# Another first batch, and branch hints on TensorE in the second MoE, in a fused FFT-mixer and two-MoE kernel

## The chip, the cores and the metric

The kernel runs on one NeuronCore of a Trainium2 chip, as one program and one launch. The metric is the device time of that launch in microseconds (us); lower is better. All engines of the core work in it: TensorE (PE in the rows; its weight loads are PEld), VectorE (DVE), ScalarE (ACT), GpSimd (POOL) and the queue of SyncE (SP), which only starts DMAs. DMAs are also started from ScalarE's and GpSimd's queues.

## What is computed

The input `x` has 8 batches of 3072 tokens of width 256. Three things follow each other:

1. A mixer along the sequence: `X = rfft(x)`, then a complex matrix product with `w_r`, `w_i` (256 x 256) and a bias, a soft threshold, and `irfft`:

```
Yr = Xr @ w_r - Xi @ w_i + b_r
Yi = Xr @ w_i + Xi @ w_r + b_i
Yr = sign(Yr) * max(|Yr| - 0.01, 0)        # and Yi alike
y  = irfft(Yr + 1j * Yi)
```

2. A dense MoE layer for all 24576 tokens, with 2048 hidden units: `h = relu(y @ w_in); x = h * h @ w_out`. Its two weights come as float64 and must be turned into float32 pairs on the chip ("decoding").

3. A routed layer: a token whose product with `w_skip` is positive goes to one of 8 experts (1024 hidden units), chosen by the largest of 8 logits; `out = x + gate * (relu(x @ w1[e]) @ w2[e])`. The other tokens are passed through.

Every product that has to be exact to float32 is made of pairs: an operand is split into a high part that TensorE's float32r reads without loss and a low rest, and three matmuls (high x high, high x low, low x high) are added up in PSUM. So an operand costs a rounding copy (ScalarE) and a subtraction (VectorE or GpSimd).

## The kernel before

The transform of a batch is done in two steps of small matrices. Step one (`s1_chunk`, 16 chunks `c`) multiplies by a 96 x 96 matrix and writes the result to a DRAM buffer `scr1`. Step two works on 12 groups `k` of two 128-row blocks each; a group passes through:

- `grp_read`: a DMA of 256 KB from `scr1` into `grd`;
- `grp_a`: four matmuls with `fw` into a PSUM bank, split by ScalarE into `xth` and by `grp_a2` (VectorE) into the rest `xtl`. `grp_a2` also forms `xs`, the sum of real and imaginary part, which `grp_a3` splits in turn (ScalarE, GpSimd);
- `grp_b`: the complex product. Three real products are used in place of four: of the sum with one matrix, and of each part with another. That is 18 matmuls of 256 columns into two banks, `both` and `own`;
- `grp_b2` (VectorE): bias plus `both`, plus `own`, the threshold (`mc` is the clamped value, `md` the difference). The four subtractions of 64 rows that give `md` also move real and imaginary rows into one 128-row operand. Then `mhi` (ScalarE) and `mlo` (GpSimd);
- `grp_c`: the inverse step, two times three matmuls with `iv` (pairs), copied by ScalarE to `v` and written by a DMA to `scr2`.

`sb_read` and `sb_tile` read `scr2` back and make the last inverse step; their result feeds the MoE.

The first batch has nothing to hide behind, so it is written out by hand inside a block in which the order of the code is the order on each engine: 16 chunks, then a loop over `k` from 0 to 14 in which iteration `k` issues `grp_a(k)`, a mixed sequence of `grp_b2(k - 2)`, a step of the decoder and `grp_a2(k)`, then `grp_a3(k)`, `grp_c(k - 3)` and `grp_b(k - 1)`. `mixed` takes the pieces of its generators in turn. After the loop come `sb_read`, seven chunks of the second batch and one `sb_tile`.

The decoder (`decode_a`, `decode_b`) works through 32 pieces of 128 x 512 words, of which the groups' loop takes one per iteration. On a piece VectorE makes `deca`, `decb`, `decw`, `decp` with integer operations, `decf` is built up by ScalarE and GpSimd, or on VectorE where `own(k)` says so, VectorE zeroes tiny values with `decw`, and the result is split into two parts, the rounding copy on VectorE or ScalarE, again by `own(k)`, the rest on GpSimd.

From then on a list of steps rules the order: for each tile of 384 tokens and each of 16 pieces `m` of the hidden layer, `l1` and, two steps later, `l2`, with the transform of the next batch put into fixed slots (`fft_schedule`). The scheduler is free outside of hand-written blocks and may move what does not depend on the rest to an earlier place.

The last stage is the routed layer, again in a hand-written order. The number of tokens of an expert is known on the chip only, so the code of an expert is a chain of up to 12 nested conditions, one per tile of 256 tokens:

```
def tiles(i):
    with tc.If((fast0 if e == 0 and i == first else n) > i * T2) as cond:
        ...
        moe2(e, *place(e, i), ...)
        if i + 1 < STATIC:
            tiles(i + 1)
```

Every engine runs each condition as a compare-and-branch of its own (L1033). While an expert has tokens left, the branch falls through to the next tile; at its end the branch is taken, past the tiles that are not needed, to the code of the next expert. Three tiles of the first expert are made ahead of the chain.

## Time and profile before

| | |
|---|---|
| median of 3 runs | 3532.19 us (3532.07 to 3536.48) |
| the profiled execution: its own time | 3548.67 us |
| its span | 3546.8 us |
| PE busy | 3431.1 us, 97% of the span |
| DVE busy | 2341.6 us, 66% |
| ACT busy | 2174.0 us, 61% |
| POOL busy | 831.0 us, 23% |

The profiled execution took 16.5 us longer than the median of the runs, and its span is 1.9 us shorter than its own time. The shares are averages over stages with different limits: in the page's line of slices PE stands at 9 (90% or more) from the third slice to the end, but at 6 and 7 in the first two, where DVE stands at 7 and 9. So the first slices and the last stage are to be read apart from the rest.

### The profile page before, as it was taken

How to read it: one execution, taken by the hardware profiler on the slowest of the kernel's cores; microseconds unless marked ns; L12 is line 12 of the kernel's file. 1: busy time of each engine (PE TensorE's matmuls, PEld its weight loads, DVE VectorE, ACT ScalarE, POOL GpSimd, SP SyncE). 2: the span in 40 equal slices, each digit the busy share in tenths (PEclk: the TensorE clock that was granted, in tenths of full speed). 3: DMA queues.
4: the chain of work that ended last, by engine and by line, in shares of the span. 5: the costliest groups of instructions: out<-in, count | busy, mean ns of one | idle time of the engine just before them, and what ended most of it. 6: DMA issues, size and time to landing. Idle time of an engine off the chain costs nothing. (4 is left out here: it accounts for less than half of the span.)

```text
span 3546.8 us, 69418 instructions
## 1 busy us (share of the span) xinstructions
PE 3431.1 (97%) x24974; PEld 3360.0 (95%) x24974; DVE 2341.6 (66%) x6851; ACT 2174.0 (61%) x4669; POOL 831.0 (23%) x808
## 2 busy tenths in 40 slices
PE   6799999999999999999999999999999998999998
PEld 4599999999999999999999999999999998999998
DVE  7956777766776677767766766777765654444444
ACT  3377766766776676676676766666777743333332
POOL 5501111221122112212221222011101234333333
PEclk8799999999999999999999999999999999999999
DMA  6532222222222122222221222111111112213221
GB/s 218 155 94 75 76 64 66 65 70 63 63 71 65 54 74 63 65 60 66 68 63 59 69 67 67 44 52 53 40 47 37 41 34 81 84 46 95 71 73 39
DMA packets 190870, 244.44 MB, mean 69 GB/s; under 512 B 32807, under 2 KB 142382, under 8 KB 190466
## 3 DMA queue, kind: packets, MB, share of 16 engines
q1 hardware_dynamic: 164770, 197.63, 19.4%
q0 software_dynamic: 18800, 32.64, 3.4%
q10 hardware_dynamic: 6896, 9.11, 0.7%
q8 instruction: 214, 3.51, 0.4%
q14 instruction: 190, 1.56, 0.2%
HBM read 124.76 MB, written 115.82 MB: 68 GB/s over the span
## 5 line engine op out<-in xcount | busy, mean ns | idle before, releaser
L461 DVE TENSOR_TENSOR glo<-r,ghi 128x384 fp32r<-128x384 f32 x1024 | 622.8, 609 | 615.4 <-ACT ghi L460 608.0
L122 PE MATMUL ps_acc<-wout,ghi 128*128 128x256 f32 x6144 | 917.8, 284 | 6.2 <-ACT ghi L460 3.6
L122 PE MATMUL ps_h<-yhi,win 128*128 128x384 f32 x4096 | 889.7, 339 | 0.4 <-ACT r L456 0.4
L122 PEld LDWEIGHTS ps_acc<-wout,ghi 128*128 128x128 f32 x6144 | 850.6, 189 | 22.2 <-ACT x L475 5.6
L486 DVE SCALAR_TENSOR_TENSOR junk<-x,wg 128x256 f32<-128x256 f32 x1701 | 812.2, 477 | 86.4 <-ACT x L475 44.1
L456 ACT ACTIVATE r<-ps_h 128x384 f32<-128x384 f32 x1024 | 503.6, 492 | 591.4 <-PE ps_h L122 493.3
L122 PEld LDWEIGHTS ps_h<-yhi,win 128*128 128x128 f32 x4096 | 675.7, 189 | 3.8 <-ACT r L456 2.0
L457 ACT ACTIVATE r<-r 128x384 f32<-128x384 f32 x1024 | 538.1, 525 | 31.7
L122 PE MATMUL ps_acc<-wout,glo 128*128 128x256 f32 x3072 | 537.7, 282 | 4.8 <-DVE glo L461 3.5
L460 ACT CAST ghi<-r 128x384 fp32r<-128x384 f32 x1024 | 525.5, 513 | 22.8 <-POOL wout L105 2.6
L122 PE MATMUL ps_h<-ylo,win 128*128 128x384 f32 x2048 | 525.8, 338 | 0.0
L122 PEld LDWEIGHTS ps_acc<-wout,glo 128*128 128x128 f32 x3072 | 439.0, 188 | 10.2 <-DVE glo L461 9.5
L630 POOL DMA_INDIRECT slots<-val,idx x192 | 191.5, 997 | 806.3 <-DVE idx L628 723.6
L122 PEld LDWEIGHTS ps_h<-ylo,win 128*128 128x128 f32 x2048 | 373.2, 188 | 0.0
L883 ACT ACTIVATE h2h<-ps_h 128x256 fp32r<-128x256 f32 x271 | 104.4, 385 | 301.7 <-PE ps_h L122 207.8
L122 PE MATMUL ps_acc<-w,h2h 128*128 128x256 f32 x1600 | 263.7, 287 | 3.8 <-ACT h2h L883 3.1
L105 POOL TENSOR_TENSOR mlo<-md,mhi 128x512 fp32r<-128x512 f32 x96 | 125.1, 1303 | 560.4 <-ACT mhi L412 523.0
L884 DVE SCALAR_TENSOR_TENSOR h2l<-ps_h,h2h 128x256 fp32r<-128x256 f32 x271 | 114.6, 424 | 207.1 <-ACT h2h L883 165.4
L122 PEld LDWEIGHTS ps_acc<-w,h2h 128*128 128x128 f32 x1600 | 220.1, 191 | 4.8 <-ACT h2h L883 4.0
L105 POOL TENSOR_TENSOR xlo<-xraw,xhi 96x512 fp32r<-96x512 f32 x96 | 128.3, 1337 | 394.0 <-ACT xhi L174 349.6
L105 POOL TENSOR_TENSOR xtl<-xs,xth 128x256 fp32r<-128x256 f32 x96 | 78.9, 822 | 486.7 <-ACT xth L372 241.8
L388 PE MATMUL ps_fft<-wm,xth 128*128 128x256 f32 x1152 | 188.8, 287 | 2.4 <-ACT xth L372 2.4
(172 smaller groups left out, 4474.7 us busy)
## 6 DMA issues: line engine op xcount, KB each, us to landing
grd<-scr SPq DMA_DIRECT2D x96, 256.0 KB
d<-scr SPq DMA_DIRECT2D x64, 384.0 KB
out_dram<-x SPq DMA_DIRECT2D x192, 128.0 KB
x1s<-x SPq DMA_DIRECT2D x192, 128.0 KB
xraw<-in_x_dram SPq DMA_DIRECT2D x125, 192.0 KB
scr<-v SPq DMA_DIRECT2D x84, 256.0 KB
scr<-s1o SPq DMA_DIRECT2D x106, 192.0 KB
wraw<-in_moe_w_dram SPq DMA_DIRECT2D x32, 256.0 KB
```

Source lines behind the costliest of these rows:

```text
L105: return engine.tensor_tensor(out=out, in0=a, in1=b, op=ALU.subtract)
L122: nc.tensor.matmul(out=out, lhsT=lhs[a], rhs=rhs[b], start=first and (a, b) == (0, 0), stop=last and pairs is then)
L388: nc.tensor.matmul(out=out_, lhsT=x[i][:, c, kb, :], rhs=w[n][j][:, kb, :], start=not (kb or i or j), stop=bool(low and kb))
L456: nc.scalar.activation(out=g, in_=p, func=AF.Relu)
L457: nc.scalar.activation(out=g, in_=g, func=AF.Square)
L460: nc.scalar.copy(out=hi, in_=g)
L461: st["step"] = nc.vector.tensor_tensor(out=lo, in0=g, in1=f32(hi), op=ALU.subtract).ins
L486: nc.vector.scalar_tensor_tensor(out=junk, in0=o, scalar=1.0, in1=st["wg"][:, e, :], op0=ALU.mult, op1=ALU.mult, accum_out=st["lg", b][:, ...
L630: ins = nc.gpsimd.indirect_dma_start(out=slots[:], out_offset=bass.IndirectOffsetOnAxis(ap=idx, axis=0), in_=val, in_offset=None, bounds_c ...
L883: nc.scalar.activation(out=hi, in_=p, func=AF.Relu)
L884: nc.vector.scalar_tensor_tensor(out=lo, in0=p, scalar=0.0, in1=f32(hi), op0=ALU.max, op1=ALU.subtract)
```

## The change

In the first batch alone (`b == 0`):

- `grp_b` uses four real products again. With the weights held as (-w_i, w_r, w_i), one matmul of 512 columns makes a part's share of both outputs; there are 12 of them in a group, into one bank. `xs` and its split fall away (`grp_a3` is not called), and so does VectorE's second addition in `grp_b2`.
- `grp_b2` makes `md` with one subtraction of 128 x 512 and leaves real and imaginary rows where they are. In their place `grp_c` multiplies half-height operands (64 of the 128 rows), with matrices `iv0` that are laid out for that: 12 matmuls of 256 columns in a group in place of 6, alternating between rows 0 to 63 and 64 to 127, into two banks, and two copies to `v` in place of one.
- The weights are split in two parts: `split_first` for the first batch, and `split_mix` (sum and difference of the weights, for the three products of the later batches) among the MoE's first steps. The matrices `iv` of the later batches are loaded into the buffers of `iv0` by 8 more DMAs of 384 KB on GpSimd's queue.
- `w_r` and `w_i` are loaded after chunk 5, the biases after the first two `grp_read`; three chunks of the second batch are loaded inside the loop.

In the decoder: `decw` is made by ScalarE (a square, compared with the square of the old bound), the rounding copy is always on ScalarE, and `own(k)` holds for even `k` below 8 and above 20. Four of the first 16 chunks' copies go from ScalarE to VectorE.

In the routed layer: each tile issues, on TensorE alone, a hint for the branch of the next tile, with the outcome computed from the number of tokens, after the fifth piece of the hidden layer.

```diff
-            ins = nc.scalar.copy(out=o.rearrange("p a b -> p (a b)"), in_=p[:96, :])
+            if early and not b and c > 8 and c % 2:
+                nc.vector.tensor_copy(out=o.rearrange("p a b -> p (a b)"), in_=p[:96, :])
+            else:
+                nc.scalar.copy(out=o.rearrange("p a b -> p (a b)"), in_=p[:96, :])
...
+        def split_first(stage):
+            for n, t in zip((1, 2), stage):
+                nc.scalar.copy(out=wm[:, n, 0], in_=t)
+                sub(nc.vector, wm[:, n, 1], t, f32(wm[:, n, 0]))
+            nc.vector.tensor_scalar(out=wm[:, 0], in0=f32(wm[:, 2]), scalar1=-1.0, scalar2=None, op0=ALU.mult)
...
-            return k < 6 or k > 20
+            return k % 2 == 0 and (k < 8 or k > 20)
...
-            ve.tensor_scalar(out=w, in0=high, scalar1=0x7FFFFFFF, scalar2=None, op0=ALU.bitwise_and)
+            nc.scalar.activation(out=f32(w), in_=high.bitcast(F32), func=AF.Square)
...
-            nc.vector.scalar_tensor_tensor(out=f, in0=w, scalar=float(0x38100000), in1=f, op0=ALU.is_ge, op1=ALU.mult)
-            yield
-            if own(k):
-                nc.vector.tensor_copy(out=dst[0], in_=f)
-            else:
-                nc.scalar.copy(out=dst[0], in_=f)
+            nc.vector.scalar_tensor_tensor(out=f, in0=f32(w), scalar=(1.125 * 2.0 ** -15) ** 2, in1=f, op0=ALU.is_ge, op1=ALU.mult)
+            yield
+            nc.scalar.copy(out=dst[0], in_=f)
...
-            both = bank(b, "fft", 3)[:, :D]
+            both = bank(b, "fft", 3)[:, :D] if b else None
             own = bank(b, "fft", 3).rearrange("p (c e) -> p c e", c=2)
-            for out_, c, n in ((both, 2, 0), (own[:, 0, :], 1, 2), (own[:, 1, :], 0, 1)):
+            if b:
+                todo = ((both, 2, wm[:, 1], None), (own[:, 0, :], 1, wm[:, 0], 0), (own[:, 1, :], 0, wm[:, 2], 1))
+            else:
+                todo = ((own, (0, 1), (wm[:, 1:3], wm[:, 0:2]), None),)
+            for out_, c, w, first in todo:
+                terms = [(c, w, kb) for kb in range(2)] if b else [(c[n], w[n], kb) for n in range(2) for kb in range(2)]
...
-            nc.vector.tensor_tensor(out=t, in0=both.unsqueeze(1).broadcast_to([128, 2, D]), in1=bias, op=ALU.add)
+            whole, part = (both.unsqueeze(1).broadcast_to([128, 2, D]), both) if b else (own, own[:, 1, :])
+            nc.vector.tensor_tensor(out=t, in0=whole, in1=bias, op=ALU.add)
...
-            nc.vector.tensor_tensor(out=t, in0=own, in1=t, op=ALU.add)
-            yield
+            if b:
+                nc.vector.tensor_tensor(out=t, in0=own, in1=t, op=ALU.add)
+                yield
...
+            else:
+                sub(nc.vector, d, t, c)
...
+                p = [psum(f"acc{(2 * k + g) % 3}", [128, 512], 1)[:, :D] for g in range(2)]
+                order = [(i, a, c) for c in range(2) for i in range(2) for a in range(2 - c)]
+                for n, (i, a, c) in enumerate(order):
+                    for g in range(2):
+                        s = slice(64 * g, 64 * g + 64)
+                        nc.tensor.matmul(out=p[g], lhsT=iv[a][s, 2 * k + i, :], rhs=m[c][s, i, :], start=n == 0, stop=n == len(order) - 1)
+                for g in range(2):
+                    nc.scalar.copy(out=v[:, g, :], in_=p[g])
...
-                if k < NK:
-                    grp_a3(0, k)
...
+                if i == 2 and NB > 1:
+                    staged = load_mix(nc.sync)
+                if i in (18, 21, 24, 27) and NB > 1:
+                    load_iv((i - 18) // 3, "iv_")
+                if i == 12 and NB > 1:
+                    split_mix(staged)
...
-                with tc.If((fast0 if e == 0 and i == first else n) > i * T2) as cond:
+                more_rows = (fast0 if e == 0 and i == first else n) > i * T2
+                with tc.If(more_rows, preferred_fallthrough_block=True, label=f"tile{e}_{i}" if i > first else None) as cond:
...
+                        between[4].append(lambda: tc.mark_branch_hint_location(f"tile{e}_{i + 1}", n > (i + 1) * T2, {ET.PE}))
```

The order of the instructions, at three places. VectorE in the loop over the groups, one iteration, before:

```order
L396 TENSOR_TENSOR mt<-ps_fft,bias 128x512
L260 TENSOR_SCALAR deca<-raws 128x256
L400 TENSOR_TENSOR mt<-ps_fft,mt 128x512
L264 SCALAR_TENSOR_TENSOR decb<-raws,deca 128x256
L402 TENSOR_SCALAR mc<-mt 128x512
L266 TENSOR_SCALAR decw<-raws 128x256
L268 TENSOR_SCALAR decp<-decb 128x256
L282 SCALAR_TENSOR_TENSOR decf<-decw,decf 128x256
L105 TENSOR_TENSOR xtl<-ps_h,xth 128x4x2x64
L105 TENSOR_TENSOR md<-mt,mc 64x256 x4
L356 TENSOR_TENSOR xs<-ps_h,xs 128x256
```

and now:

```order
L421 TENSOR_TENSOR mt<-ps_fft,bias 128x512
L272 TENSOR_SCALAR deca<-raws 128x256
L428 TENSOR_SCALAR mc<-mt 128x512
L276 SCALAR_TENSOR_TENSOR decb<-raws,deca 128x256
L107 TENSOR_TENSOR md<-mt,mc 128x512
L281 TENSOR_SCALAR decp<-decb 128x256
L295 SCALAR_TENSOR_TENSOR decf<-decw,decf 128x256
L107 TENSOR_TENSOR xtl<-ps_h,xth 128x4x2x64
```

The second addition (L400), `decw` and `xs` are gone, the four pieces of `md` are one, and `md` stands ahead of `xtl`.

TensorE at the same place, from the inverse step of one group to the first matmuls of another, before:

```order
L122 MATMUL ps_acc_659<-mhi,iv_88 128x256
L122 MATMUL ps_acc_659<-mhi,iv_89 128x256
L122 MATMUL ps_acc_659<-mlo,iv_88 128x256
L388 MATMUL ps_fft<-wm,xth 128x256 x4
L388 MATMUL ps_fft<-wm,xtl 128x256 x2
L340 MATMUL ps_h<-fw,grd 128x128 x4
```

(the first three lines stand twice in a group, the next two three times) and now, from the middle of the inverse step:

```order
L461 MATMUL ps_acc_676<-mhi,iv_89 128x256
L461 MATMUL ps_acc_677<-mhi,iv_89 128x256
L461 MATMUL ps_acc_676<-mlo,iv_88 128x256
L461 MATMUL ps_acc_677<-mlo,iv_88 128x256
L409 MATMUL ps_fft<-wm,xth 128x512 x8
L409 MATMUL ps_fft<-wm,xtl 128x512 x4
L350 MATMUL ps_h<-fw,grd 128x128 x4
```

The inverse step alternates between two banks, and the complex product has fewer and wider matmuls.

TensorE in a tile of the routed layer, between two pieces of the hidden layer, now:

```order
L124 MATMUL ps_h<-xt2h,w_00_34827 128x256
L124 MATMUL ps_h<-xt2h,w_01_34828 128x256
L124 MATMUL ps_h<-xt2l,w_00_34827 128x256 x2
L1097 REGISTER_ALU
L1136 BRANCH_PREFETCH_HINT
L124 MATMUL ps_acc_38329<-w_00_34829,h2h 128x256
```

The two rows without a matmul are new; before, the matmuls follow one another there.

## Rows read from the trace of the kernel before

**Rows 1.** Busy time by stretch: stretch, length, engines busy (instructions), PEclk, DMA share, GB/s

```profile
0.00:39.50 39.50, 19.24 (x32) 5.85 (x32) 24.99 (x59) 13.12 (x22) 15.82 (x25) 0.87 0.89 287
53.50:120.40 66.90, 47.76 (x287) 42.74 (x286) 66.25 (x128) 26.64 (x63) 42.88 (x50) 0.86 0.40 126
120.40:134.90 14.50, 8.50 (x42) 7.39 (x41) 13.98 (x26) 3.57 (x8) 8.15 (x9) 0.74 0.40 127
134.90:169.20 34.30, 24.98 (x62) 13.41 (x62) 28.34 (x69) 10.40 (x21) 16.75 (x21) 0.65 0.70 211
2934.70:3537.80 603.10, 574.48 (x4728) 571.97 (x4728) 272.86 (x625) 202.94 (x486) 215.16 (x210) 0.97 0.24 68
```

**Rows 2.** Timeline of DVE, one group: start, us, engine, line, operation, shapes

```profile
83.39 0.68 DVE L105 TENSOR_TENSOR xtl<-ps_h,xth 128x512 fp32r<-128x512 f32 x1
83.99 2.14 DVE L105 TENSOR_TENSOR md<-mt,mc 64x256 f32<-64x256 f32 x4
86.16 0.42 DVE L356 TENSOR_TENSOR xs<-ps_h,xs 128x256 f32<-128x256 f32 x1
86.50 0.68 DVE L396 TENSOR_TENSOR mt<-ps_fft,bias 128x512 f32<-128x512 f32 x1
87.10 1.18 DVE L260 TENSOR_SCALAR deca<-raws 128x256 uint32<-128x256 uint32 x1
88.20 0.68 DVE L400 TENSOR_TENSOR mt<-ps_fft,mt 128x512 f32<-128x512 f32 x1
...
89.14 0.95 DVE L402 TENSOR_SCALAR mc<-mt 128x512 f32<-128x512 f32 x1
90.01 0.41 DVE L266 TENSOR_SCALAR decw<-raws 128x256 uint32<-128x256 uint32 x1
```

**Rows 3.** Timeline of POOL, in that group

```profile
86.86 1.27 POOL L105 TENSOR_TENSOR mlo<-md,mhi 128x512 fp32r<-128x512 f32 x1 [1.88 <-ACT mhi L412]
```

**Rows 4.** Timeline of PE: a forward step, and a step of the first MoE

```profile
54.29 1.05 PE L340 MATMUL ps_h<-fw,grd 128*128 128x128 f32 x8
...
179.32 0.87 PE L122 MATMUL ps_h<-yhi,win 128*128 128x384 f32 x4
...
180.38 0.88 PE L122 MATMUL ps_acc<-wout,ghi 128*128 128x256 f32 x6
...
181.45 0.86 PE L122 MATMUL ps_h<-yhi,win 128*128 128x384 f32 x4
```

**Rows 5.** Timeline from the last group to the first MoE's steps

```profile
134.91 0.62 ACT L412 CAST mhi<-md 128x512 fp32r<-128x512 f32 x1 [3.04 <-DVE md L105]
...
147.93 3.70 PE L438 MATMUL ps_fft<-sb,d 96*128 96x96 f32 x16 [4.25 <-DMA sb<-in_sb_dram]
...
169.22 1.13 DVE L461 TENSOR_TENSOR glo<-r,ghi 128x384 fp32r<-128x384 f32 x1
```

**Rows 6.** Timeline of PE: the first matmuls of two tiles that follow one another

```profile
3242.83 0.64 PE L122 MATMUL ps_h<-xt2h,w 128*128 128x256 f32 x4
...
3254.68 0.63 PE L122 MATMUL ps_h<-xt2h,w 128*128 128x256 f32 x4
```

**Rows 7.** Waits of PE from 3000 to 3530: total us, times, longest

```profile
PE ps_h L122 <- issue: 10.0, 2, 7.0
PE ps_fft L122 <- PEq L1033: 6.9, 2, 3.8
PE ps_h L122 <- PEq L1033: 6.3, 2, 3.2
PE ps_h L122 <- DVEq L1033: 3.5, 1, 3.5
```

**Rows 8.** The branch's line from 3255 to 3275: duration ns min/median/max, first and last start

```profile
L1033 PEldq COMPARE_BRANCH  x3: 65/197/3563, 3265.4 to 3269.5; - x3
```

**Rows 9.** Busy time in the 10 us after a wait (first and last of seven)

```profile
3014.16:3024.16 10.00, 10.00 (x64) 10.00 (x65) 4.63 (x9) 4.33 (x10) 2.73 (x3) 0.73 0.56 173
...
3524.22:3534.22 10.00, 10.00 (x72) 10.00 (x73) 2.55 (x6) 2.69 (x7) 2.89 (x3) 0.83 0.19 40
```

More of the change, by code (lines that the diff above doesn't have):

```diff
@@ L79, in _constants @@
     s1 = s1.reshape(96, 96)
+    iv0 = iv.reshape(NG // 2, 2, 2, 64, 128).transpose(1, 3, 0, 2, 4).reshape(128, NG, 128)
     iv = iv.reshape(NG, 128, 128).transpose(1, 0, 2)
@@ L82, in _constants @@
     out = {}
-    for name, m in (("s1", s1), ("iv", iv)):
+    for name, m in (("s1", s1), ("iv", iv), ("iv0", iv0)):
         hi = _round12(m)
@@ L204, in split_mix @@
             sub(nc.vector, diff, i, r)
-            for n, t in enumerate((r, diff, total)):
+            for n, t in ((0, total), (2, diff)):
                 nc.scalar.copy(out=wm[:, n, 0], in_=t)
@@ L211, in load_fw, with load_iv @@
             queue.dma_start(out=fw[:, 6 * q:6 * q + 6], in_=A["fw"][:, 6 * q:6 * q + 6])
-        def load_iv(q):
+        def load_iv(q, name="iv0_"):
             for i, k in enumerate(("hi", "lo")):
-                nc.gpsimd.dma_start(out=iv[i][:, 6 * q:6 * q + 6], in_=A["iv_" + k][:, 6 * q:6 * q + 6])
+                nc.gpsimd.dma_start(out=iv[i][:, 6 * q:6 * q + 6], in_=A[name + k][:, 6 * q:6 * q + 6])
         win = [const.tile([128, 2, DFF], F32R, name=f"win{i}", tag=f"big{4 + i}") for i in range(2)]
@@ L346, in grp_a @@
             xv = [t[:, :2].rearrange("p c k (g j) -> p (k g) c j", g=2) for t in x]
-            xs = sbuf("xs", [128, 4, 64], F32)
             nc.scalar.copy(out=xv[0], in_=pv)
-            nc.scalar.copy(out=xs, in_=pv[:, :, 0, :])
+            xs = None
+            if b:
+                xs = sbuf("xs", [128, 4, 64], F32)
+                nc.scalar.copy(out=xs, in_=pv[:, :, 0, :])
             st["xt", b, k] = x, xv, xs, pv
@@ L355, in grp_a2 @@
             yield
-            nc.vector.tensor_tensor(out=xs, in0=pv[:, :, 1, :], in1=xs, op=ALU.add)
+            if b:
+                nc.vector.tensor_tensor(out=xs, in0=pv[:, :, 1, :], in1=xs, op=ALU.add)
             real = None
@@ L364, in grp_a2 @@
                     nc.vector.tensor_scalar(out=first, in0=f32(first), scalar1=0.0, scalar2=None, op0=ALU.mult)
-                first = xs.rearrange("p (k g) j -> p k g j", g=2)[:, :, 0, 0:1]
-                nc.vector.tensor_scalar(out=first, in0=first, scalar1=0.0, scalar2=None, op0=ALU.mult)
-            st["xt", b, k] = x, xs, real
+                if b:
+                    first = xs.rearrange("p (k g) j -> p k g j", g=2)[:, :, 0, 0:1]
+                    nc.vector.tensor_scalar(out=first, in0=first, scalar1=0.0, scalar2=None, op0=ALU.mult)
+            st["xt", b, k] = (x, xs, real) if b else (x, real)
         def grp_a3(b, k):
@@ L374, in grp_a3, with first_bins @@
             st["xt", b, k] = x, real
+        def first_bins(out_, real, c):
+            for h in range(2):
+                mm3(nc, out_[0:1], [real[:, i, c, h:h + 1] for i in range(2)], [wm[:, 1, i, h, :] for i in range(2)], False, False)
         def grp_b(b, k):
             x, real = st.pop(("xt", b, k))
-            w = [[wm[:, n, i] for i in range(2)] for n in range(3)]
-            both = bank(b, "fft", 3)[:, :D]
+            both = bank(b, "fft", 3)[:, :D] if b else None
             own = bank(b, "fft", 3).rearrange("p (c e) -> p c e", c=2)
-            for out_, c, n in ((both, 2, 0), (own[:, 0, :], 1, 2), (own[:, 1, :], 0, 1)):
+            if b:
+                todo = ((both, 2, wm[:, 1], None), (own[:, 0, :], 1, wm[:, 0], 0), (own[:, 1, :], 0, wm[:, 2], 1))
[3 more added lines that the diff above has]
+                terms = [(c, w, kb) for kb in range(2)] if b else [(c[n], w[n], kb) for n in range(2) for kb in range(2)]
                 for low, pairs in enumerate((((0, 0), (0, 1)), ((1, 0),))):
-                    for kb in range(2):
-                        if low and kb and real is not None and n:
-                            for h in range(2):
-                                mm3(nc, out_[0:1], [real[:, i, 1 - c, h:h + 1] for i in range(2)], [t[:, h, :] for t in w[0]], False, False)
+                    for n, (c_, w_, kb) in enumerate(terms):
                         for i, j in pairs:
-                            nc.tensor.matmul(out=out_, lhsT=x[i][:, c, kb, :], rhs=w[n][j][:, kb, :],
-                                             start=not (kb or i or j), stop=bool(low and kb))
+                            rhs = w_[:, j, kb, :] if b else w_[:, :, j, kb, :]
+                            nc.tensor.matmul(out=out_, lhsT=x[i][:, c_, kb, :], rhs=rhs, start=not (n or i or j),
+                                             stop=bool(low and n == len(terms) - 1))
+                        if low and n == 0 and real is not None:
+                            for r in range(2) if not b else () if first is None else (first,):
+                                first_bins(out_ if b else own[:, r, :], real, r)
             st["p", b, k] = both, own
@@ L730, in fft_mixer_moe_kernel @@
                     grp_b(0, k - 1)
-                if NB > 1 and NK - 1 <= k < NK + 3:
-                    ld(1, k - NK + 1)
+                if NB > 1 and k in (4, 6, 8):
+                    ld(1, k // 2 - 2)
+            if NB > 1:
+                ld(1, 3)
             sb_read(0, 0)
```

37 lines of the change are left out of this document (22 added, 15 removed).

## The prediction

> **What bounds the kernel now.** I read the busy time by stretch first, since the page's averages hide the stages [rows 1]. From 53.5 to 120.4 us, where nine groups of the first batch pass, VectorE is busy 66.25 of 66.90 us and TensorE 47.76: the loop is VectorE's, 66.90 / 9 = 7.43 us a group. In the last stage, from 2934.7 to 3537.8, TensorE is busy 574 of 603 us at a granted clock of 0.97: that stage is TensorE's, with holes. Between the two, some 2700 us of dense MoE are TensorE's without holes, and the change leaves them alone. So two stages decide, each by its own limit.
>
> The timeline of VectorE shows where a group's 7.4 us go [rows 2]; start to start is what an instruction costs there, since VectorE never idles. `md` takes 83.99 to 86.16 = 2.17 us, `xs` 0.34, the second addition (L400) 0.61, `decw` some 0.3 of its 0.41. `deca` takes 1.10 from its start at 87.10 to the next start, and ends at 88.28: just after GpSimd's `mlo`, which ran from 86.86 to 88.13 [rows 3]. So part of VectorE's time is waiting for GpSimd inside an instruction.
>
> In the routed layer one tile costs TensorE 3254.68 - 3242.83 = 11.85 us when nothing is in the way [rows 6]. The stage has 4728 matmuls [rows 1], a tile 100 (48 per layer and 4 transposes), so 47 tiles, which would take 557 us. It took 603: 46 us are lost. The waits of TensorE name where [rows 7]: 10.0 + 6.9 + 6.3 + 3.5 = 26.7 us in seven waits, one at the end of each expert but the last. The rows name L1033, the branch, and the branch itself shows it [rows 8]: it takes 65 ns when it falls through, and 3563 ns once, where it is taken. So a taken branch stops TensorE's sequencer for 3.6 us, of which some 3.3 are seen as a wait (the sequencer runs a little ahead). After each such wait the engine is slow as well: in the 10 us behind it the granted clock is 0.73 in the first of seven cases and 0.83 in the last [rows 9], where 1.00 is 2.4 GHz and 0.50 is 1.2 GHz; that is 10 x 0.27 = 2.7 and 1.7 us lost, 2.2 on the mean. Seven times 2.2 and 26.7 make 42 of the 46 us.
>
> **The loop over the groups.** VectorE loses `xs` 0.34, L400 0.61, `decw` 0.33, and `md` shrinks from 2.17 to one 128 x 512 operation, priced like `xtl`, 0.60 (83.39 to 83.99) [rows 2]. Left: 7.43 - 1.28 - 1.57 = 4.6 us for the group shown, if the waits for GpSimd stay as long as they are.
>
> TensorE gets more work. From the first MoE's steps: 9 matmuls of 256 columns in 181.45 - 180.38 = 1.07, so 0.119 each, 6 of 384 in 1.06, so 0.177 [rows 4]; on that line 512 columns cost 0.235 (an estimate; no row has that width in float32r). The complex product goes from 18 x 0.119 = 2.1 to 12 x 0.235 = 2.8. The forward step stays at about 0.9 [rows 4]. The inverse step goes from 6 to 12 matmuls: no row has half-height ones, so they lie between 6 x 0.119 = 0.7, as if two halves ran at once, and 12 x 0.119 = 1.4. I take 1.4, the nearest row being a whole matmul of that width. Sum: 0.9 + 2.8 + 1.4 = 5.1 at full clock. TensorE therefore becomes the limit of the loop, not VectorE. The clock was 0.86 there [rows 1], with TensorE idle a third of the time; with hardly any idle time I take 0.95: 5.4 us a group. The Trainium skill (TensorEngine Tiling (Array Packing), Key Properties) says that tiles of different rows run matmuls in parallel, and that a change of the tiling mode drains the engine. By it the inverse step would cost 0.7 and two drains, the loop would be VectorE's again at 4.6 to 4.8 us, and the sum 6 us better; no row here can show it.
>
> ScalarE had 26.6 of 66.9 us in the loop [rows 1]: it loses `xs` and its split and gets a square and a second copy, about the same. GpSimd had 42.9, 4.8 a group; it loses the rest of `xs` and gets 8 DMA starts in all, so it stays under 5.4. Two of these DMAs wait for TensorE's inverse step in front of `mlo`; the step is due earlier anyway, so I cost them nothing, and if they block, GpSimd is the next limit.
>
> Nine groups gain 9 x (7.43 - 5.4) = 18. The first two groups gain little (1). The end, 14.5 us [rows 1], shrinks to two complex products, one inverse step and VectorE's last chain, 2.8 + 1.4 + 2.8 + 0.6 + 0.4 + 0.6 = 8.7, a gain of 6. Together 25.
>
> **Ahead of the loop.** Three raw pieces of 256 KB no longer stand ahead of the first group's read: 0.8 MB at 287 GB/s [rows 1], 2.7 us. Against it, squares in ScalarE's queue wait for raw pieces and hold chunk copies behind them, though VectorE takes four of those. I take 1.5 gained, between 3 lost and 3 gained.
>
> **Behind the loop.** From the last group to the first `glo` are 34.3 us [rows 1, 5], in which the eleven last pieces are decoded on VectorE. Now a piece costs it `deca` 1.10, `decb` 0.33, `decp` 0.2 and the zeroing 0.34, about 2.1 with half an `own` operation: 23, and 2.4 for four operations of the new `split_mix`, which the scheduler pulls forward to here. So 26 in place of 34. ScalarE comes close to that now with its squares, copies and rounding, so I take a gain of 6, not 8. The chain of data cannot gain more than this: from `mhi` at 134.91 to the last inverse step at 147.93, 13 us [rows 5], a DMA to DRAM and back, stays. The dense MoE is costed at nothing.
>
> **The routed layer.** If the hint makes the target ready in time, the branch costs what one that falls through does. The hint stands behind the fifth of eight pieces, about half a tile or 6 us ahead of the branch, longer than the 3.6 us. Its two instructions cost about what a branch does, 65 ns, 47 times, hidden as long as the sequencer is ahead. I keep 9.5 of the 42 us: one of the seven waits was 7.0 long [rows 7], two blocks in a row, of which the hint covers one (3.7 and 2.2 for the slow clock), and one was ended by VectorE's own branch (3.5), which gets no hint. Gain 32.
>
> **The sum.** 25 + 1.5 + 6 + 32 = 64.5 us. Against the profiled execution's 3548.7 that gives 3484; the runs' median is 16.5 lower, and I carry the difference over: 3532.2 - 64.5 = **3468 us**.
>
> **Rivals.**
> *The hints do nothing.* For it: no hint ran in the kernel before, so nothing shows that one shortens a branch; against it: a hint knows the target 6 us ahead. The loop's 32.5 us stay: 3500. The Trainium skill (Runtime: NRT & Kernel Launch, Instruction fetch mechanics) says that instructions are prefetched in sequence only and that a taken branch out of the present blocks stalls for a fetch; the 3563 ns agree with the second half, and by the first this rival would be right. Chance 0.17.
> *The pairs run at once*, 4.7 us a group: 9 x 0.7 = 6 better, 3462. Chance 0.15.
> *The loop is held* by a clock that stays low, by GpSimd's queue or by the 3 MB that the 8 extra loads add to it: 6.6 us a group, 11 us lost, and 2 more ahead or behind: 3481. For it: 0.86 and 0.40 of DMA share [rows 1] while less was asked. Chance 0.12.
> *Slower.* The block that a hint fetches takes the place of the one that TensorE runs into next. Then tiles that fall through stall as the taken ones did, 3.3 us and 2.2 of slow clock, up to 40 times: 40 x 5.5 = 220, less 32.5 of the first batch: 3720. It decides against the change from six such stalls on (32.5 / 5.5). Against it: the hint is computed from the count, and says "not taken" on these 40. Chance 0.03.
>
> **How the numbers follow.** My forecast, 3450 to 3486 on its own, has 0.50; with the two cases inside that stretch, 0.77. The range reaches up to the first rival and a little over it, and down to the pairs with all seven waits gone: 3446 to 3506. A measurement of this kernel tells 0.2%, about 7 us, from no change. Faster 0.95, the same 0.02, slower 0.03.
>
> **What would show it.** In the loop: starts of `xtl` 5.4 us apart, TensorE without idle time, VectorE with some. 12 matmuls of the inverse step in 1.4 us, or in 0.7. `glo` for the first time near 136 in place of 169. In the last stage: taken branches on TensorE well under 1 us, waits behind L1033 nearly gone, the clock at 1.00. I am wrong if the taken branch still takes 3.5 us, if a branch that falls through takes more than 65 ns, or if `xtl` stays at 7 us.

## The result: 0.85% faster, under half of what was forecast

| | before | changed |
|---|---|---|
| median | 3533.4 us (4 runs) | 3503.6 us (4 runs: 3501.6 to 3507.5) |
| ratio | 1 | 0.9916, 95% interval 0.99 to 0.9932 |
| profiled execution, span | 3546.8 us | 3505.7 us |

The gain is 30 us where 64.5 were forecast, and 3504 lies in the upper end of the range. The stages of the changed kernel first, with the same columns as [rows 1]: the prologue, nine groups of the loop, the end of the loop, the stretch from the last `mhi` to the first `glo`, the routed layer.

```profile
0.00:38.70 38.70, 21.80 (x32) 6.38 (x32) 16.29 (x40) 13.68 (x29) 12.77 (x22) 0.81 0.84 263
56.10:105.00 48.90, 46.50 (x296) 38.12 (x295) 42.12 (x74) 25.16 (x63) 37.27 (x45) 0.97 0.71 217
105.00:113.60 8.60, 6.11 (x39) 4.12 (x37) 8.46 (x13) 3.59 (x11) 6.61 (x8) 0.97 0.70 193
113.60:152.50 38.90, 26.20 (x68) 14.48 (x69) 26.36 (x56) 17.88 (x44) 21.91 (x30) 0.63 0.78 227
2914.50:3496.00 581.50, 565.16 (x4724) 563.72 (x4725) 274.08 (x624) 204.13 (x486) 217.18 (x211) 0.99 0.24 71
```

Nine groups take 48.90 us, 5.43 each (before 7.43), and TensorE is busy 46.50 of them. The end of the loop takes 8.6 in place of 14.5. But the stretch behind the loop has grown from 34.3 to 38.9 us, and its DMA share stands at 0.78. The timeline of TensorE in a group, and its first complex product:

```profile
46.03 3.75 PE L409 MATMUL ps_fft<-wm,xth 128*128 128x512 f32 x8 [3.52 <-DVE real L376]
...
67.42 1.05 PE L350 MATMUL ps_h<-fw,grd 128*128 128x128 f32 x8
68.40 0.74 PE L461 MATMUL ps_acc<-mhi,iv 64*128 64x256 f32 x8
68.97 0.40 PE L461 MATMUL ps_acc<-mlo,iv 64*128 64x256 f32 x4
69.30 2.14 PE L409 MATMUL ps_fft<-wm,xth 128*128 128x512 f32 x8
71.28 1.10 PE L409 MATMUL ps_fft<-wm,xtl 128*128 128x512 f32 x4
```

Twelve half-height matmuls take 0.90 us (68.40 to 69.30). The first part of the first complex product takes 3.75 us where the same eight matmuls later take 2.14; the granted clock was 0.50 (1.2 GHz) there, behind a wait of 3.52 us. The stretch behind the loop, from the timeline of all engines:

```profile
113.60 0.38 SPq L197 DMA_DIRECT2D stage<-in_w_r_dram  x1
113.61 0.62 ACT L442 CAST mhi<-md 128x512 fp32r<-128x512 f32 x1 [1.63 <-DVE md L107]
117.50 0.54 POOL L227 DMA_DIRECT2D iv<-in_iv_hi_dram  x1 [0.67 <-PE ps_acc L461]
122.95 0.33 SPq L469 DMA_DIRECT2D d<-scr  x1
128.31 3.70 PE L479 MATMUL ps_fft<-sb,d 96*128 96x96 f32 x16 [4.47 <-DMA sb<-in_sb_dram]
141.12 0.18 DVE L627 TENSOR_SCALAR val<-tokid 128x24 uint32<-128x24 f32 x1 [5.96 <-DMA tokid<-in_tokid_dram]
152.49 1.09 DVE L502 TENSOR_TENSOR glo<-r,ghi 128x384 fp32r<-128x384 f32 x1
```

The chain of data starts 21.3 us earlier than before (113.61 against 134.91 [rows 5]), but the first `glo` only 16.7 earlier (152.49 against 169.22; the prediction looked for it near 136). From the eighth `glo` to the 512th the lead is a steady 14.5 to 15.0 us.

In the routed layer, the waits of TensorE and its branches at two ends of an expert (the waits' columns are us in all, times, longest; the branch's row has the smallest, median and largest duration in ns; PEq and DVEq are the sequencers of TensorE and VectorE, and "issue" is time in which the engine waited for nothing that the profile shows):

```profile
PE ps_h L124 <- DVEq L1084: 9.2, 4, 3.6
PE ps_fft L124 <- PEq L1084: 3.2, 1, 3.2
PE ps_h L124 <- issue: 2.6, 1, 2.6
PE ps_fft L124 <- DVEq L1084: 1.1, 1, 1.1
```

```profile
L1084 PEldq COMPARE_BRANCH  x3: 65/192/380, 3161.0 to 3162.6; - x3
L1084 PEldq COMPARE_BRANCH  x3: 73/186/3761, 3407.4 to 3411.7; - x3
```

The taken branch, 3563 ns in [rows 8], takes 380 ns. That holds for seven of nine; a second branch in a row takes 2065, and the seventh, near 3407, still 3761. The seven waits are 16.1 us in place of the 26.7 of [rows 7], and five of them now name VectorE's sequencer (DVEq).

### The profile page after: what moved, and what is told of

Its sections match the earlier page's. It is cut to its first block, busy times and chain, and to the rows that moved or that the text cites. A ratio compares the mean times of both kernels' runs of the same rounds, so it can differ in the third digit from the quotient of the medians.

```text
span 3505.7 us, 69465 instructions
## 1 busy us (share of the span) xinstructions
PE 3421.7 (98%) x24974; PEld 3344.7 (95%) x24974; DVE 2302.6 (66%) x6739; ACT 2184.7 (62%) x4711; POOL 829.1 (24%) x812
## 5 line engine op out<-in xcount | busy, mean ns | idle before, releaser
L124 PEld LDWEIGHTS ps_acc<-wout,glo 128*128 128x128 f32 x3072 | 439.6, 189 | 11.2 <-DVE glo L502 10.5
L409 PE MATMUL ps_fft<-wm,xth 128*128 128x256 f32 (+1 forms) x1104 | 187.6, 294 | 3.5 <-DVE real L376 3.5
L107 POOL TENSOR_TENSOR xtl<-xs,xth 128x256 fp32r<-128x256 f32 x84 | 67.8, 807 | 485.0 <-ACT xth L386 229.9
```

Of the source, the lines that this page charges most:

```text
L107: return engine.tensor_tensor(out=out, in0=a, in1=b, op=ALU.subtract)
L124: nc.tensor.matmul(out=out, lhsT=lhs[a], rhs=rhs[b], start=first and (a, b) == (0, 0), stop=last and pairs is then)
L409: nc.tensor.matmul(out=out_, lhsT=x[i][:, c_, kb, :], rhs=rhs, start=not (n or i or j), stop=bool(low and n == len(terms) - 1))
```

## Experiments

Each ratio is to the kernel before on the same chip, with its 95% interval. "First glo" (its start) and "routed" (from the start of the last `glo` to the end) are from the run's profile, in us.

| run | median | before there | ratio | first glo | routed |
|---|---|---|---|---|---|
| changed kernel | 3503.6 | 3533.4 | 0.9916 (0.99 to 0.9932) | 152.5 | 637.9 |
| h_only | 3517.4 | 3536.4 | 0.995 (0.9936 to 0.9963) | 170.9 | 635.9 |
| no_hints | 3533.4 | 3536.4 | 0.9994 (0.9985 to 1.0003) | 153.2 | 662.4 |
| hints3 | 3505.7 | 3536.4 | 0.9917 (0.9903 to 0.9931) | 150.7 | 638.8 |
| hold_val | 3505.7 | 3536.4 | 0.9922 (0.9908 to 0.9935) | 150.1 | 636.6 |
| before_again | 3535.5 | 3538.0 | one run | 169.4 | 654.7 |
| hold_iv | 3501.7 | 3538.0 | 0.9896 (0.9879 to 0.9912) | 145.3 | 637.7 |
| hold_mix | 3504.2 | 3538.0 | 0.9904 (0.9888 to 0.9921) | 153.0 | 636.3 |
| no_pairs | 3505.1 | 3538.0 | 0.9904 (0.9888 to 0.9921) | 152.5 | 637.3 |
| read_q | 3508.2 | 3539.1 | 0.9916 (0.9902 to 0.9929) | 153.4 | 637.8 |
| late_hint | 3522.3 | 3539.1 | 0.996 (0.9947 to 0.9973) | 151.4 | 654.2 |
| best | 3505.9 | 3539.1 | 0.9904 (0.9889 to 0.9919) | 147.6 | 638.3 |
| before12 | 3557.5 | 3548.7 | 1.0029 (1.0019 to 1.0039) | 170.0 | 672.0 |
| h_only12 | 3539.7 | 3548.7 | 0.9977 (0.9967 to 0.9986) | 171.1 | 655.2 |
| after_same | 3508.6 | 3539.2 | 0.9916 (0.9902 to 0.9929) | 154.7 | 638.7 |
| hold_iv2 | 3501.8 | 3539.2 | 0.9895 (0.988 to 0.991) | 148.4 | 635.9 |

### The two halves of the change

h_only is the kernel before with the hints:

```diff
-                with tc.If((fast0 if e == 0 and i == first else n) > i * T2) as cond:
+                more_rows = (fast0 if e == 0 and i == first else n) > i * T2
+                with tc.If(more_rows, preferred_fallthrough_block=True, label=f"tile{e}_{i}" if i > first else None) as cond:
...
+                        between[4].append(lambda: tc.mark_branch_hint_location(f"tile{e}_{i + 1}", n > (i + 1) * T2, {ET.PE}))
```

> The kernel before with the branch hints alone, first batch untouched. Two readings of the measured 29.9 us. (A) The two profiled executions are typical: from the last glo to the end they differ by 665.2 - 637.9 = 27.3 us, so the hints alone give some 27 us, 3506, ratio 0.992, and the first batch next to nothing. (B) The profiled execution of before was a long one in its routed layer (3548.7 against a median of 3533.4, 15 us); in an ordinary execution the hints give 29.9 less the 15 us that the first batch shows at the eighth glo, so 15 us, 3518, ratio 0.9957. In both, a taken branch of TensorE drops from 3.6 to about 0.4 us.

no_hints takes the same lines out of the changed kernel.

> The changed kernel without the hints. By (A) 3530, ratio 0.999, by (B) 3518, ratio 0.9957. In either, the profile up to the last glo is that of the changed kernel (first glo near 152.5, 64th near 329), the taken branches of TensorE take 3.4 to 4 us again, and their seven waits 25 us or so.

In h_only eight of the nine taken branches take 0.37 to 0.48 us, the second in a row 2.16, and the seven waits are 13.8 us. The hints alone give 18 us by the ratio (19 by the medians), near the 15 of (B). But the first batch alone gives 2 us, with an interval from a gain of 5 to a loss of 1, though its profile is 13 to 15 us ahead at the last `glo` (2866.3 against 2879.1 and 2881.6 in two profiles of the kernel before); and the waits in no_hints are 33 us, not the 25 expected. Neither reading holds as it stood: 18 and 2 don't make 30. The hints are worth more on the changed kernel, 0.9994 - 0.9916, or 28 us. The kernel before, once more:

> The kernel before, unchanged, for a second profile. The hints alone gave 19 us (3536.4 to 3517.4), the first batch alone 3 (3533.4), and both some 30. The first profile of before needs 665.2 us from the last glo to its end, and its own time is 12 us above the median of its runs. If that profile was a long execution, this one needs about 653 us there, all of the difference in the waits at the ends of the experts or in the clock behind them; then the hints gain 18 on the kernel before and 26 on the changed one, whose taken branches cost more without them. If it needs 665 again, the first batch must be what differs, with a last glo near 2870 in place of 2881.6.

It takes 654.7 us behind the last `glo`, 10.5 less than the first profile, so the profile that the prediction was made from was a long one in just this layer. The waits were the same, 26.0 us against 26.7:

```profile
PE ps_h L122 <- PEq L1033: 9.1, 3, 3.3
PE ps_h L122 <- issue: 7.0, 1, 7.0
PE ps_fft L122 <- PEq L1033: 6.4, 2, 3.3
PE ps_h L122 <- DVEq L1033: 3.5, 1, 3.5
```

but in the 10 us behind them the clock was higher, 0.83 to 0.86 in all seven, where the first profile has 0.66 to 1.00 and a mean of 0.78 (two of the seven in [rows 9]). That is 4 us; the rest of the 10.5 lies elsewhere in the layer, whose mean clock was 0.97 against 0.96. On the chip of before12 (below) the kernel before takes 3548.7 us in 19 runs, as the first profile did; the chips differ.

### The place of the code

Without hints the routed layer of the changed kernel takes 662.4 us, 7.7 more than that of the kernel before, for the same code. The timeline of TensorE in no_hints shows an end of an expert with two waits, one of them behind a single matmul:

```profile
3247.36 0.36 PE L124 MATMUL ps_h<-xt,w 128*128 128x256 f32 x1 [2.83 <-PEq L1083]
3251.06 1.22 PE L124 MATMUL ps_h<-xt,w 128*128 128x256 f32 x4 [3.34 <-issue]
```

TensorE's program has 40756 recorded instructions ahead of the first of these branches in the kernel before, 40768 in the changed one. So the code of the layer lies 12 instructions further on. before12 moves it by as much and changes nothing else:

```diff
+            if b == 0 and k0 == 0:
+                for _ in range(6):
+                    nc.tensor.matmul(out=rk[:, :8], lhsT=tri, rhs=ohf[:, :8], start=True, stop=True)
             nc.tensor.matmul(out=rk, lhsT=tri, rhs=ohf, start=True, stop=True)
```

> The kernel before with six tiny matmuls (128 x 8, with their weight loads 12 instructions of TensorE) ahead of a matmul of the first batch's routing, whose result is then overwritten. Up to its first branch TensorE runs 40756 instructions in the kernel before and 40768 in the changed one without hints, 12 more, which shifts the whole code of the routed layer by 12. Theory of placement: the routed layer costs what it costs in the changed kernel without hints, 662 us in place of 654.7, with waits at the ends of the experts of some 33 us in place of 26, three of them in two pieces (at the third, fifth and seventh end), and the time rises by 6 to 9 us (ratio 1.002). Rival: where the code lies doesn't matter, and the longer routed layer of the changed kernel without hints comes from what its first batch left behind (buffers, other queues): 654.7 again, ratio 1.000.

Six matmuls that take 0.7 us by themselves (from 563.3 to 564.1) make the kernel 8.8 us slower (1.0029), and the double wait is there at the same end, the fifth taken branch, as it is at the third and seventh:

```profile
3270.91 0.36 PE L122 MATMUL ps_h<-xt,w 128*128 128x256 f32 x1 [3.15 <-PEq L1036]
3275.03 1.22 PE L122 MATMUL ps_h<-xt,w 128*128 128x256 f32 x4 [3.77 <-issue]
```

The Trainium skill (Runtime: NRT & Kernel Launch, Instruction fetch mechanics) says that instructions come in blocks of 256. A branch that lands on the last instructions of a block would then wait for the next block as well; that is a conclusion, not on the page. One matmul between the two waits fits it, but no run shows where the blocks begin. The same with the hints, as h_only12:

> The kernel before with the hints and the same six tiny matmuls. With the hints alone all nine taken branches of TensorE took under 0.5 us (and one second branch 2.2); in every build of the changed kernel with hints the branch at the end of the seventh expert took 3.5 to 3.9 us. If that is the placement of the code (12 instructions further), this branch takes 3.5 us or more here too, the waits add up to 16 in place of 13.8 us, and the time rises by 2 to 4 us against the hints alone. If it stays at 0.4, something else in the changed kernel makes it miss.

```profile
L1034 PEldq COMPARE_BRANCH  x3: 65/186/389, 3418.5 to 3420.2; - x3
L1037 PEldq COMPARE_BRANCH  x3: 73/186/3505, 3438.1 to 3442.1; - x3
```

The first row is h_only, the second h_only12, at the seventh taken branch: 389 ns becomes 3505. That is the branch that stays slow in every build of the changed kernel. So the place decides that as well; why the hint fails there stays open. The time moved by more than expected (0.995 to 0.9977, some 9 us on another chip), which this one branch doesn't explain: the waits of over 1 us are 19.9 in place of 13.8, not the 16 expected, and some of the new ones name ScalarE or no engine. It also leaves a question: on that chip the hints gain 17.9 us on the shifted kernel (3557.5 to 3539.7), as much as on the kernel that is not shifted (18, on another chip). So the shift alone doesn't explain the 28 us that they gain on the changed kernel.

### What a hint does

late_hint moves the hint from behind the fifth step of a tile to behind the tenth (`between[9]`).

> The changed kernel with TensorE's hint after the tenth step of a tile in place of the fifth, so about 1 us or less ahead of the branch in place of 7.8. If a hint starts a fetch that takes the 3.3 to 4.2 us of a taken branch without a hint, the taken branches cost 2 to 3.5 us here in place of 0.4, the seven waits add up to some 24 us again and the time rises by 8 to 20 us (3512 to 3524). If the hint only tells the branch which way to go, and the code is there anyway, the branches stay at 0.4 us and the time at 3504.

All nine taken branches are long again, 3.4 to 4.7 us, though a hint stands 1.7 us ahead of eight of them (the second of the two in a row has none so near):

```profile
L1084 PEldq COMPARE_BRANCH  x3: 73/197/4278, 3163.7 to 3168.5; - x3
L1084 PEldq COMPARE_BRANCH  x3: 72/202/3617, 3491.5 to 3495.6; - x3
```

Of the 16 us that are lost against the changed kernel (0.996 against 0.9916) 11.7 are waits (27.8 against 16.1). So a hint doesn't just tell the branch which way to go: it has to come early. That it starts a fetch fits this, but isn't shown: such a fetch with 1.7 us of start would have left 2 to 3.5 us of the branch, as expected, and a hint that comes 1.7 us ahead didn't save even these 1.7. Between 1.7 and 7.8 us nothing was tried. The Trainium skill (same section) says that instructions are prefetched in sequence only. In the changed kernel seven of nine taken branches with a hint 7.8 us ahead took 0.37 to 0.47 us, so the rule does not cover a hinted branch.

hints3 gives VectorE and ScalarE the same hints.

> The changed kernel with the same hints on VectorE and ScalarE too. If what is left of the waits at the ends of the experts (16.1 us) is VectorE's own taken branch (two waits of 3.4 and 3.6 us are put down to it, against 1.1 where it comes in time), these two fall to about 1.1 and the time by 5 to 7 us, to 3497, ratio 0.990. If the waits are TensorE's own, or if a hint costs VectorE and ScalarE as much in the 40 tiles that fall through as it saves in seven, the time stays at 3503 or rises.

Nothing moved. VectorE still keeps TensorE waiting five times, twice for 3.5 us (four of the five are in the first row):

```profile
PE ps_h L124 <- DVEq L1084: 9.3, 4, 3.5
PE ps_fft L124 <- PEq L1084: 3.4, 1, 3.4
```

That VectorE is most of what is left is shown by the releaser; why it is late, why its hint doesn't help, and whether one elsewhere would, is open.

### Behind the loop

hold_val, hold_mix and hold_iv each hold back one thing that the scheduler had pulled into this stretch:

```diff
-            ve.tensor_tensor(out=pos, in0=base, in1=slot0, op=ALU.add)
+            with tc.issue_after(st["step"]):
+                ve.tensor_tensor(out=pos, in0=base, in1=slot0, op=ALU.add)
...
-                    staged = load_mix(nc.sync)
+                    with tc.issue_after(st["sp"].ins):
+                        staged = load_mix(nc.sync)
...
-                    load_iv((i - 18) // 3, "iv_")
+                    with tc.issue_after(st["pool"]):
+                        load_iv((i - 18) // 3, "iv_")
```

(`val` as `pos`, and `split_mix` behind `st["step"]`.)

> The changed kernel with two small VectorE operations of the routing (val, which reads tokid, and pos) held back to their place in the program, instead of standing in VectorE's queue in the middle of the decoding, where val waits 6.0 us for tokid's load (135.2 to 141.1). If that wait sets the end of the decoding, the first glo comes 4 to 6 us earlier (147 to 148 in place of 152.5) and the time falls by as much, to 3498. If the pieces of the raw weights come late anyway (their loads stand behind the read of scr2 in SP's queue and share the DMA engines with the 3 MB of iv), the wait moves to them and the time falls by less than 1.5 us.

> The changed kernel with the loads of w_r and w_i for split_mix held behind the read of scr2 in SP's queue, and split_mix's VectorE operations held behind the MoE's first steps. In the changed kernel these 0.5 MB are issued at 113.6 us, right ahead of the last writes to scr2, and six VectorE operations stand in the tail (118.3 to 126, some 4 us). If they delay the tail, the first glo comes 3 to 4 us earlier and the time falls by as much. If not, nothing moves by more than 2 us, or split_mix now stands in the way of the first MoE steps and the eighth glo is later.

> The changed kernel with the eight reloads of iv (3 MB) held behind the last of the decoder's GpSimd operations, so that none runs inside the loop or up to the read of scr2. If these DMAs are what eats the gain behind the loop (DMA share 0.81 to 0.92 between 110 and 130 us against 0.32 to 0.36 before; the read of scr2 is issued 9.4 us after the last mhi, before 6.3), that distance falls back to 6 to 7, the raw pieces land earlier, the first glo comes at 146 to 148 in place of 152.5, and the time falls by 4 to 6 us. If the tail is set by the order in SP's queue and by the decoder itself, the first glo stays within 2 us, and so does the time.

Without `val` in its queue VectorE waits 4.8 us at the same place, now for GpSimd's part of a decoded piece (GpSimd waits 6.2 us for ScalarE there, and ScalarE 3.2 for a raw piece):

```profile
139.28 0.42 DVE L283 SCALAR_TENSOR_TENSOR decf<-raws,decp 128x256 f32<-128x256 uint32 x1 [4.83 <-POOL wout L107]
```

The first `glo`, at 150.1, lies 0.6 us below the spread of the builds that don't touch this stretch (150.7 to 154.7). hold_mix does nothing that can be told from this spread either. hold_iv does: the read of `scr2` is issued 6.5 us behind the last `mhi` in place of 9.3, and the whole stretch is as long as before, 34.4 us:

```profile
110.91 0.62 ACT L442 CAST mhi<-md 128x512 fp32r<-128x512 f32 x1 [1.64 <-DVE md L107]
117.43 0.33 SPq L469 DMA_DIRECT2D d<-scr  x1
133.87 0.21 DVE L627 TENSOR_SCALAR val<-tokid 128x24 uint32<-128x24 f32 x1 [2.39 <-DMA tokid<-in_tokid_dram]
145.28 1.09 DVE L502 TENSOR_TENSOR glo<-r,ghi 128x384 fp32r<-128x384 f32 x1
```

Since executions differ by some us here, the two stood side by side once more:

> The changed kernel itself, beside hold_iv on the same chip. Earlier it stood at a ratio of 0.9916 [0.99, 0.9932] to the kernel before, hold_iv at 0.9896 [0.9879, 0.9912], in different calls. It should repeat 0.991 to 0.992.

> hold_iv again, beside the changed kernel. If the 7.4 us that its profile showed from the eighth glo on belong to the held reloads, it comes out 5 to 8 us below the changed kernel here too, with the first glo at 145 to 147 against 150 to 153.5. If they were the luck of one execution (other builds of the changed kernel spread from 150.1 to 153.2 there), the two are within 2 us.

```profile
112.16 0.62 ACT L442 CAST mhi<-md 128x512 fp32r<-128x512 f32 x1 [1.63 <-DVE md L107]
118.64 0.33 SPq L469 DMA_DIRECT2D d<-scr  x1
148.37 1.09 DVE L502 TENSOR_TENSOR glo<-r,ghi 128x384 fp32r<-128x384 f32 x1
```

The read is issued 6.5 us behind the last `mhi` again (9.7 in after_same), and the stretch takes 36.2 us (38.3 in after_same). hold_iv2 is 6.8 us below the changed kernel (3501.8 against 3508.6), its first `glo` 6.3 earlier. But its profile, taken of its longest run, is only 0.7 us ahead of after_same's at the 64th `glo`, and hold_iv lies only 2.5 and 3.4 us below hold_mix and no_pairs, two other builds of the changed kernel on its chip. So the reloads of `iv` hold the read of `scr2` by some 3 us, and they are 2.5 to 7 us of the missing gain; how much is open. hold_iv has the lowest ratio here, 0.9895 and 0.9896 of the kernel before.

read_q adds to hold_iv that the first reads of `scr2` are issued from GpSimd's queue:

```diff
-            st["sp"] = nc.sync.dma_start(out=d4, in_=scr2[b]
+            st["sp"] = (nc.sync if b or t > 1 else nc.gpsimd).dma_start(out=d4, in_=scr2[b]
```

> The changed kernel with the reloads of iv held back as in hold_iv, and the first two reads of scr2 (d4) moved from SP's queue to GpSimd's, so that the loads of the raw pieces no longer stand behind reads that wait for the last writes to scr2. In hold_iv SP issues no raw piece from 108.5 to 118.7 us, and the next but one at 121.2 and 126.6. If this order sets the end of the decoding, the raw pieces are issued 4 to 6 us earlier, the first glo comes at 140 to 142 in place of 145.3, and the time falls by 3 to 5 us against hold_iv (ratio 0.9885). If the reads now hold GpSimd's queue, which has three operations of every decoded piece, for the same time, the first glo stays at 145 or comes later and the time does not fall.

The wait went along: GpSimd's queue idles 4.5 and 4.0 us in front of the two reads, the decoder with it, and the first `glo` is at 153.4 again:

```profile
118.67 0.58 POOL L469 DMA_DIRECT2D d<-scr  x1 [4.47 <-ACT wm L218]
126.83 0.56 POOL L469 DMA_DIRECT2D d<-scr  x1 [3.97 <-PE ps_fft L479]
```

So whether SP's order holds the raw pieces couldn't be told apart. best holds back all three:

> The changed kernel with three things held back: the reloads of iv behind the decoder (as in hold_iv), the loads for split_mix behind the first read of scr2 (as in hold_mix), and val and pos at their place (as in hold_val). Alone, hold_iv moved the first glo from 152.5 to 145.3 and the others moved it by nothing that can be told from the spread of the profiles (150.1 to 153.2). If the tail is now a chain in which the loads of w_r and w_i and val's wait (2.4 us in hold_iv) stand, the first glo comes at 142 to 143 and the time 2 to 3 us below hold_iv's, ratio 0.989; otherwise it stays at 145 and 0.9896.

It does no better than hold_iv: the first `glo` comes at 147.6, between the 145.3 and 148.4 of hold_iv's two profiles, and the interval of its ratio takes theirs in. In all three VectorE stands still once more before the MoE runs evenly, 6.4 us here (162.5 to 168.9), 4.0 and 6.2 in the other two; in the changed kernel no `glo` there waits longer than 1.6.

### The half-height matmuls

no_pairs lets `grp_c` do the six of one half and then the six of the other, by exchanging the loops over `g` and over `order`.

> The changed kernel with the half-height matmuls of grp_c in two blocks of six, rows 0 to 63 first and then 64 to 127, in place of alternating. In the changed kernel the 12 take 0.90 us (68.40 to 69.30), against 1.4 if they ran one after the other at 0.119 and 0.7 if in pairs. If alternating rows is what lets them overlap, the 12 take 1.4 us here and a group of the loop 5.4 to 5.9 us (VectorE and GpSimd have some room), the time rises by 0 to 5 us. If a half-height matmul is short by itself, the 12 take 0.9 us again and nothing changes.

```profile
68.96 0.85 PE L461 MATMUL ps_acc<-mhi,iv 64*128 64x256 f32 x6
69.53 0.28 PE L461 MATMUL ps_acc<-mlo,iv 64*128 64x256 f32 x1
...
70.20 2.14 PE L409 MATMUL ps_fft<-wm,xth 128*128 128x512 f32 x8
```

The twelve take 1.24 us (68.96 to 70.20) in place of 0.90, so the pairs do run at once. In the changed kernel's trace they start 3 to 4 ns apart (68.399 and 68.402, 68.621 and 68.625, 68.739 and 68.742), a pair every 0.117 us; six pairs are 0.70, and 0.1 goes at either end, from 68.40 to the second pair and behind the last. The Trainium skill (TensorEngine Tiling (Array Packing), Key Properties) says as much: different tiles can run matmuls in parallel, and a change of the mode drains the engine. In no_pairs too, the second half's first matmul starts while the first half is still at work (at 69.30), so that the loss is 0.34 us a group and not the 0.5 of twelve in a row. The kernel's time does not show it.

## Why the forecast was too high

| term | forecast | measured |
|---|---|---|
| prologue and first two groups (third `xtl`: 53.48, now 56.12) | 2.5 | -2.6 |
| nine groups (53.48 to 120.37, now 56.12 to 104.98) | 18 | 18.0 |
| end of the loop (to the last `mhi`: 134.91, now 113.61) | 6 | 5.9 |
| last `mhi` to the first `glo` (34.3, now 38.9) | 6 | -4.6 |
| first `glo` to the 512th | 0 | -1.9 |
| 512th to the last `glo` (1316.3 in before_again, now 1319.9) | 0 | -3.6 |
| routed layer (654.7 in before_again, now 637.9) | 32 | 16.8 |
| sum | 64.5 | 28.0 |

The sum of the profiles' terms stands beside 29.9 by the medians. The rows that name before_again take the second profile of the kernel before; by the first, the last two would be -1.0 and 27.3.

**The loop was right to the tenth, by a sum that was not.** TensorE's work in a group was forecast as 0.9 + 2.8 + 1.4 and is 1.0 + 2.9 + 0.9 = 4.8 us; the second rival (the pairs run at once) had the last term. The group takes 5.43 all the same: from 56 to 105 us VectorE waits 6.8 us for TensorE, in six waits, and TensorE in its turn is idle 5%. A clock of 0.95 was taken, 0.97 came. So the 18.0 is in part luck: too much work and too little idle time made up for each other. (The six terms for the end of the loop add up to 8.6, not 8.7; 8.63 was measured.)

**The first groups** lost where they were to gain. The first complex product starts 0.3 us later than before and takes 7.0 us in place of 5.7, and then TensorE waits 1.1 us for the next `grd`. It has more work than before, and its first 3.6 us ran at a granted clock of 0.50 (first row; the second is the product before, up to the next forward step; columns as [rows 1]):

```profile
46.03:49.58 3.55, 3.54 (x8) 2.78 (x9) 2.48 (x6) 1.18 (x3) 3.20 (x6) 0.50 1.12 403
45.73:51.27 5.54, 5.39 (x31) 4.43 (x32) 3.65 (x9) 1.94 (x5) 4.86 (x7) 0.69 0.84 266
```

The prediction had counted half speed nowhere ahead of the loop.

**"26 in place of 34" behind the loop was a wrong step.** It set VectorE's work against the length of the stretch, as if VectorE set the end. The work came out as forecast, 26.36 us, but before it was 28.34 of 34.30 us [rows 1], not 34: VectorE was not without idle time there even before. Now it stands still for 12.5 of 38.9 us, 6.0 for the load of `tokid`, most of the rest for GpSimd and ScalarE; ScalarE in its turn waits 4.8 us for raw pieces. The stretch is a chain (last `mhi`, write and read of `scr2`, the loads queued behind that read, the decoding), and the prediction had priced only its first 13 us. Without the reloads it takes 34.4 and 36.2 us in two profiles, with them 38.9 and 38.3; so the forecast gain of 6 is missing even without them. These 3 MB appear in the prediction only in a rival, as a load on the loop; in the rows the read of `scr2` behind it is issued 3 us later with them.

**The routed layer** failed twice. First, the 42 us were taken from one execution, on a slow chip or moment: 26.0 us of waits were there in the second profile too, but only 11 of slow clock (10 us times 0.14 twice and 0.17 five times) in place of 15, and the layer as a whole was 10.5 us shorter. I had carried the 16.5 us between the profile and the median over to the sum as if they lay outside of the terms; most lay inside this one. Second, "9.5 of the 42 stay" was too little: 22 stayed, 16.1 of waits and 6.2 of slow clock. The mechanism was right, 3.6 us became 0.38. But once TensorE's branch is short, VectorE's chain ends last: 1.07 us at best, 3.4 and 3.6 where VectorE's signal came later, for a reason that no row shows. The prediction saw that once, in the one wait that was VectorE's already, and not that it stands behind four others. And the seventh branch didn't take the hint.

The clock rows behind a wait show what a shorter wait can give back (changed kernel, same columns as [rows 9]: behind waits of 3.44, 1.07, 3.59 and 3.23 us):

```profile
3030.89:3040.89 10.00, 10.00 (x72) 10.00 (x73) 5.34 (x11) 4.78 (x12) 5.20 (x6) 0.83 0.88 283
3236.04:3246.04 10.00, 10.00 (x85) 10.00 (x86) 5.90 (x12) 5.98 (x14) 6.92 (x7) 1.00 0.90 286
3298.98:3308.98 10.00, 10.00 (x63) 10.00 (x64) 4.63 (x9) 4.29 (x10) 5.37 (x5) 0.72 0.87 266
3411.89:3421.89 10.00, 10.00 (x85) 10.00 (x86) 6.79 (x13) 5.84 (x14) 6.20 (x6) 1.00 0.95 289
```

Behind all three waits of 1.07 and 1.08 us the clock stayed at 1.00; but it did so behind the 3.23 us of the seventh branch too, so the length of a wait isn't all that decides.

**The parts don't add up.** The prediction costed the first batch and the hints as independent. Without hints the routed layer of the changed kernel is 7.7 us longer, which takes back most of the first batch's 12.8 (both against before_again), and a shift of the code by 12 instructions alone brings such a loss (8.8 us). With hints the layer is only 2 us longer than in h_only (637.9 against 635.9), with one slow branch; why h_only12 loses some 9 is open. Of the rivals, "the hints do nothing" came nearest in time (3500) but by luck, for its mechanism is wrong: the hints give 18 to 28 us.

## What to carry to other kernels

A wait that several engines share is worth only the distance to the engine that is next; look up when each of the others is ready before the whole wait is booked as a gain. Where a tail is a chain of transfers, price its links, not the engine that is busiest in it, and look at what the scheduler pulls into it. Take stalls from more than one execution, and where branches are taken, measure a variant that only shifts the code before a small gain is put down to an edit elsewhere.

## What the runs showed of the hardware

- A hint 7.8 us ahead brings a taken branch of TensorE from 3.4 to 4.2 us down to 0.37 to 0.5, eight of nine with one placement of the code and seven of nine with another; 1.7 us ahead it brings nothing. On VectorE and ScalarE no effect on the time was seen (0.9917 against 0.9916).
- Six matmuls of 8 columns, far from the branches, that move the code by 12 instructions cost 8.8 us, with second waits at three taken branches.
- A pair of half-height matmuls (256 columns) of different halves takes the 0.117 us of one whole matmul (0.119, [rows 4]).
- One of the chips ran the kernel before at 3548.7 us, the others at 3533 to 3539.
